# Gelu on four W1 items at once and silu on two W2 items at once, in a fused attention and MLP kernel

## The chip, the core and the metric

The kernel runs on one core of a Trainium2 chip. A core has five engines with their own in-order instruction queues, which meet through semaphores: TensorE (PE, matmuls; PEld are its weight loads), VectorE (DVE), ScalarE (ACT), GpSimd (POOL) and SyncE (SP, which here issues all DMAs). The metric is the device time of one execution in microseconds; lower is better.

## The reference

```python
def _A_ref(x, wqkv, wo):                      # 32 heads of 32, sequence 2048, width 1024
    q, k, v = split(x @ wqkv)
    p = softmax(q @ k.T * 32 ** -0.5)
    return (p @ v) @ wo

def _B_ref(x, w1, b1, w2, b2):                # hidden width 3584
    y = _layernorm(x)
    h = gelu(y @ w1 + b1)                     # tanh form
    return h @ w2 + b2

xn = _layernorm(A_x)
return A_x + _A_ref(xn, ...) * silu(_B_ref(xn, ...))
```

All tensors are bf16, x is 2048 x 1024. Two chains hang on the normalized x: an attention block and an MLP. Their product, added to x, is the output.

## The kernel before

**A planner writes the order.** The kernel does not call the engines directly. Each piece of work is an operation with an engine, a cost, a priority and tokens that it reads and writes (`dve`, `act`, `dma`, `chunk`, lines 580 to 601). `_Plan.run` (line 93) then simulates the engines with these costs and fixes the order of every queue, and `settle` (390) derives the semaphore waits. So a changed cost or dependency can move any instruction behind it. The costs of DVE and ACT are linear in the elements with a fixed part (`c_ps`, `c_f32`, `c_b16`, `c_b4`, `c_act`, `c_acts`, lines 552 to 568).

**Attention** is done for 8 groups of 4 heads (w = 0 to 7), each with 8 blocks of 256 queries and 8 units of 256 keys. A unit is 8 score matmuls on PE (L811, into 6 of the 8 PSUM banks), two exponentials of 128 x 1024 on ACT (L820, tile P), and the matmuls of P with the values (L605). DVE adds up the exponentials for the softmax sums (L837 and L854, tiles PA and PR). Scores have the first claim on PE: other work is placed so that it ends before ACT would run dry, by a guard.

**The MLP** goes through the rows in 8 chunks of 256. Its PE work is cut into items which take one of the other two PSUM banks in turn, together with projections, values and the output projection.

- `make_y` (970) loads x again, normalizes it on DVE and transposes it by DMA into yT.
- A W1 item (`w1_item`, 981; 14 to a chunk) is 16 matmuls for 256 hidden columns. DVE then adds b1 from the PSUM bank into half of a tile xb (L992, 128 x 512), which frees the bank. After every second item the gelu of both is done on 1024 elements per partition: three operations on DVE (L1001 to L1003), a tanh on ACT (L1004), two more on DVE (L1005, L1008). The last writes two of the 20 slots of hT. There are two xb and two ut tiles, so two pairs can be under way.
- A W2 item (`w2_item`, 1014; 4 to a chunk) is 56 matmuls that read the 14 hT slots of its chunk. DVE forms z from the bank (L1029, 128 x 512), ACT takes its tanh (L1033, with an f32 result), DVE forms the product (L1034), and a DMA stores it to a scratch tensor in DRAM (L1036). All three tiles z, zh, g exist twice, in gw.

`seq_mlp` (1043) gives the order: W1 of the first chunk, and then for each chunk its four W2 items with six W1 items of the next chunk between them (2 after each of the first three), and the other eight W1 items of the next chunk. `mlp(10.0, 450.0)` (1113) spreads this over positions among the 512 units of attention. The planner opens a W2 item only when all DVE operations that it depends on have started in the plan, and any item only when its PSUM evacuation waits for nothing but the item itself (lines 295 to 298). Priorities: exponentials go before tanh on ACT (0 and 1) unless a tanh has waited 2500 ns; on DVE bank evacuations have 0, gelu 3, pair sums 3.2.

hT is used for three things: staged x at the start, the hidden values, and at the end staged rows of x and of the stored silu results (lines 1190 to 1203). gw holds normalized x at the start and f32 intermediates in the last rows (1230).

In the last group (w = 7) the output projection items (L1215) run, their results are multiplied with the silu results and added to x on DVE (L1223, L1226), and stored.

Of the kernel before, what the change touches and what calls it, by code (L numbers as in the profile page):

```python
# [6 lines left out]
ACT = mybir.ActivationFunctionType  # L7
ALU = mybir.AluOpType
BF16 = mybir.dt.bfloat16
F32 = mybir.dt.float32  # L10
# [445 lines left out]
def bass_recurrent_scan__mha_block__mixer_channel_mlp__prompt_kernel(  # L456
# [16 lines left out]
    NW1 = FB // 2  # L473
    EPS = 1e-5
    SCALE = 32 ** -0.5
    GC, GA = 0.7978845608028654, 0.044715
# [11 lines left out]
    with ExitStack() as st:  # L488
        def sb(name, shape, dt):
            return st.enter_context(nc.sbuf_tensor(name, list(shape), dt))  # L490

        g_d = nc.dram_tensor("g_scratch", (S, D), BF16).ap()
        o_d = nc.dram_tensor("o_scratch", (HG, 128, S), BF16).ap()

        NP, NPX, NPA, NH, NW1R, NW2R = 10, 16, 3, 20, 3, 4
# [12 lines left out]
        hT = sb("hT", [128, NH, 2, 256], BF16)  # L508
# [3 lines left out]
        w2r = sb("w2r", [128, NW2R, 7, 256], BF16)  # L512
        b2b = sb("b2b", [128, D], BF16)
        b1T = sb("b1T", [128, FB], BF16)
        xb_t = [sb(f"xb{i}", [128, 2, 512], BF16) for i in range(2)]
        ut_t = [sb(f"ut{i}", [128, 2, 512], BF16) for i in range(2)]
        gw = sb("gw", [128, 4096], BF16)
        z_t = [gw[:, i * 2048:i * 2048 + 512] for i in range(2)]
        g_t = [gw[:, i * 2048 + 512:i * 2048 + 1024] for i in range(2)]
        zh_t = [gw[:, i * 2048 + 1024:i * 2048 + 2048].bitcast(F32) for i in range(2)]  # L520
        nt_t = sb("nt", [128, 256], F32)
        nv_t = [sb(f"nv{i}", [128, 256], F32) for i in range(2)]
        nr_t = sb("nr", [128, 8], F32)
# [16 lines left out]
        xnb = [gw[:, i * 1024:(i + 1) * 1024] for i in range(4)]  # L540
        iota_i = ut_t[0][:].rearrange("p a b -> p (a b)")[:, 0:256].bitcast(I32)

        def bank(i, lo=0, hi=512):
            return ps[:, i * 512 + lo:i * 512 + hi]
# [7 lines left out]
        def c_ps(n):  # L552
            return 77 + 1.0417 * n

        def c_f32(n):
            return 67 + 1.0417 * n

        def c_b16(n):
            return 67 + 0.521 * n

        def c_b4(n):
            return 67 + 0.2605 * n
# [4 lines left out]
        def c_acts(n):  # L567
            return 82 + 0.8334 * n
# [11 lines left out]
        def dve(fn, occ, R, W, prio, item=None, extra=()):  # L580
            o = add("DVE", fn, occ, DL, R, W, prio, extra=extra)
            if item is not None:
                linked(o, item)
            return o

        def act(fn, occ, R, W, prio, item=None):
            o = add("ACT", fn, occ, AL, R, W, prio)
            if item is not None:
                linked(o, item)
            return o  # L590
# [4 lines left out]
        def dma(sem, fn, nbytes, R, W, prio=3, extra=(), rate=290.0, occ=430, lat=2500.0):  # L595
            return add("SP", fn, occ, lat, R, W, prio, sem=sem, nbytes=nbytes, extra=extra, rate=rate)
# [148 lines left out]
        def after(tokens, of):  # L745

            got = []
            for x in of:
                w = plan.last_w.get(x)
                got += ([w] if w is not None else []) + plan.readers.get(x, [])  # L750
            for x in tokens:
                plan.readers.setdefault(x, []).extend(got)
# [197 lines left out]
                plan.dense["proj"].append(it)  # L950


        nw2 = {"n": 0}
        ut_n = {"n": 0}
        mq = plan.dense["mlp"]

        def load_w1(p):
# [22 lines left out]

        def w1_item(c, pi):
            p = c * NW1 + pi
            gi, hs, half = p % NW1R, p % NH, pi % 2
            ui = (p // 2) % 2
            it = _Item("mlp")
            for f2 in range(2):
                for dc in range(DC):
                    def fn(e, b, f2=f2, dc=dc):
                        return mm(e, bank(b, f2 * 256, (f2 + 1) * 256), w1r[:, gi, dc, f2 * 128:f2 * 128 + 128], yT[:, dc, :],
                                  dc == 0 and f2 == 0, dc == DC - 1)  # L990
                    chunk(it, fn, Q256, [("w1", gi), ("yT", 0), ("yT", 1)])
            dve(lambda e: e.tensor_tensor(xb_t[ui][:, half].rearrange("p (k t) -> p k t", k=2),  # L992
                                          bank(it.bank).rearrange("p (k t) -> p k t", k=2),
                                          b1T[:, 2 * pi:2 * pi + 2].unsqueeze(2).to_broadcast([128, 2, 256]), op=ALU.add),
                c_ps(512), [("b1",)], [("xb", ui, half)], 0, it)
            if half == 0:
                return it
            xs = [("xb", ui, 0), ("xb", ui, 1)]
            fl = lambda t: t[:].rearrange("p a b -> p (a b)")
            u_ = fl(ut_t[ui])  # L1000
            dve(lambda e: e.tensor_tensor(u_, fl(xb_t[ui]), fl(xb_t[ui]), op=ALU.mult), c_b16(1024), xs, [("ut", ui)], 3)  # L1001
            dve(lambda e: e.tensor_scalar(u_, u_, GA, 1.0, op0=ALU.mult, op1=ALU.add), c_b4(1024), [("ut", ui)], [("ut", ui)], 3)
            dve(lambda e: e.tensor_tensor(u_, u_, fl(xb_t[ui]), op=ALU.mult), c_b16(1024), [("ut", ui)] + xs, [("ut", ui)], 3)  # L1003
            act(lambda e: e.activation(u_, u_, ACT.Tanh, scale=GC), c_acts(1024), [("ut", ui)], [("ut", ui)], 1)  # L1004
            dve(lambda e: e.tensor_scalar_add(u_, u_, 1.0), c_b4(1024), [("ut", ui)], [("ut", ui)], 3)  # L1005
            h0 = (p - 1) % NH
            if h0 + 1 < NH:
                dve(lambda e: e.tensor_tensor(hT[:, h0:h0 + 2].rearrange("p s k t -> p (s k t)"), u_, fl(xb_t[ui]), op=ALU.mult),  # L1008
                    c_b16(1024), [("ut", ui)] + xs, [("h", h0), ("h", h0 + 1)], 3)
            else:  # L1010
                raise AssertionError
            return it

        def w2_item(c, q):
            n = c * 4 + q
            zi = n % 2
            it = _Item("mlp")
            for r in range(4):
                wi = w2slot[(c, q, r)]
                for t2 in range(2):  # L1020
                    for f in range(7):
                        def fn(e, b, r=r, t2=t2, f=f, wi=wi):
                            fb = r * 7 + f
                            hs = (c * NW1 + fb // 2) % NH
                            return mm(e, bank(b, t2 * 256, (t2 + 1) * 256), hT[:, hs, fb % 2, t2 * 128:t2 * 128 + 128],
                                      w2r[:, wi, f, :], r == 0 and f == 0 and t2 == 0, r == 3 and f == 6)
                        chunk(it, fn, Q256, [("w2", wi), ("h", (c * NW1 + (r * 7 + f) // 2) % NH)])
            cs = slice(q * 256, (q + 1) * 256)
            dve(lambda e: e.scalar_tensor_tensor(z_t[zi].rearrange("p (t n) -> p t n", t=2),  # L1029
                                                 bank(it.bank).rearrange("p (t n) -> p t n", t=2), 0.5,  # L1030
                                                 b2b[:, cs].unsqueeze(1).to_broadcast([128, 2, 256]), op0=ALU.mult, op1=ALU.add),
                c_ps(512), [("b2",)], [("z", zi)], 0, it)
            act(lambda e: e.activation(zh_t[zi], z_t[zi], ACT.Tanh, scale=0.5), c_acts(512), [("z", zi)], [("zh", zi)], 1)  # L1033
            dve(lambda e: e.scalar_tensor_tensor(g_t[zi], zh_t[zi], 1.0, z_t[zi], op0=ALU.add, op1=ALU.mult),  # L1034
                c_f32(512), [("zh", zi), ("z", zi)], [("g", zi)], 3)
            dma(f"g{zi}", lambda e: e.dma_start(g_d[c * 256:(c + 1) * 256, cs].rearrange("(t p) n -> p t n", p=128),  # L1036
                                                g_t[zi].rearrange("p (t n) -> p t n", t=2)), 131072,
                [("g", zi)], [("g_d", c, q)])
            return it

        w2slot = {}
# [65 lines left out]
            after([("w2", i)], [("P", 13 + k, h) for k in range(3) for h in range(2) if k * 2048 < (i + 1) * 1792  # L1107
                                and (k + 1) * 2048 > i * 1792])
        after([("h", k) for k in range(NH)], [XS(t) for t in range(NXS)])
        after([(k, i) for i in range(2) for k in ("z", "zh", "g")], [("xnb", t) for t in range(4)])  # L1110

        proj(1, 0)
        mlp(10.0, 450.0)
# [10 lines left out]
        for w in range(HG):  # L1124
# [23 lines left out]
            for qb in range(NQB):  # L1148
                if w == 0 and qb < 2:
                    continue  # L1150
                g = w * NQB + qb
# [35 lines left out]
                for t2 in range(2):  # L1187
                    tb = 2 * qb + t2
                    ri = tb % 3 if tb < 12 else tb - 9
# [9 lines left out]
                    xr, gr = xg[:, 0:1024], xg[:, 1024:2048]  # L1199
# [4 lines left out]
                    for nh in range(2):  # L1204
                        late = qb == NQB - 1
                        it = _Item("wo", 64 * 7 + 8 * qb + 4 * t2 + 2 * nh)
                        i2 = 2 * t2 + nh
                        sl_ = slice(nh * 512, (nh + 1) * 512)
                        if late:
                            most = _Item("wo", it.pos + 64)  # L1210
# [11 lines left out]
                        if not late:  # L1222
# [7 lines left out]
                        xf = gw[:, i2 * 1024:(i2 + 1) * 1024].bitcast(F32)  # L1230
                        dve(lambda e, most=most, gr=gr, sl_=sl_, xf=xf: e.scalar_tensor_tensor(
                            xf, bank(most.bank), 0.5, gr[:, sl_], op0=ALU.mult, op1=ALU.mult),
                            c_ps(512), [("gr", ri, nh)], [("xf", i2)] + [(k, t2) for k in ("z", "zh", "g")], 0, most)
                        dve(lambda e, xr=xr, sl_=sl_, xf=xf: e.tensor_tensor(xf, xf, xr[:, sl_], op=ALU.add),
                            c_f32(512), [("xr", ri, nh)], [("xf", i2)], 2)
                        if i2:
# [84 lines left out]
```

## Time and profile before

| | |
|---|---|
| time, median of 3 runs | 1042.89 us (1042.58 to 1043.29) |
| span of the profiled execution | 1042.1 us, 0.8 us less than that median; its own time with what lies around the span is not given apart |
| ACT busy | 1017.7 us (98%), 1129 instructions |
| PE busy | 1008.8 us (97%) |
| DVE busy | 958.4 us (92%), 1450 instructions |
| mean granted clock of TensorE | 0.998 |
| DMA, mean over the span | 161 GB/s |

The profile is of one execution. Times are microseconds unless marked ns; L820 is line 820 of the kernel. A group of instructions is shown as line, engine, operation, names of the tiles written and read, their shapes, the count, then busy time in us, the mean duration of one in ns, and the idle time of the engine just before them with what ended it. A wait row reads "who waited <- for whom: us in total, times, longest". The chain of work goes back from the last instruction to whatever released each step; its pieces are given by start and length. Matmuls are pipelined, so a busy PE is not PE at its peak.

### The profile page before, as it was taken

The numbers are of one execution on the slowest core, as the hardware profiler recorded it, in microseconds if no ns is written. First come the engines' busy times: TensorE is split into PE (matmuls) and PEld (weight loads), VectorE is DVE, ScalarE is ACT, GpSimd is POOL, SyncE is SP. The second block draws the span as 40 slices with busy tenths as digits, with TensorE's granted clock in tenths as the row PEclk, the third lists the DMA queues.
The fourth block names the chain that finished last, engine by engine and source line by source line (L and its number), as shares of the span: only waits on it lengthen the run. The fifth ranks groups of instructions, "written<-read, shape, count | busy, mean of one in ns | idle before, by whom it ended". The sixth has DMA issues, their size and how long they took to land.

```text
span 1042.1 us, 31753 instructions
## 1 busy us (share of the span) xinstructions
PE 1008.8 (97%) x14179; PEld 640.8 (61%) x14179; DVE 958.4 (92%) x1450; ACT 1017.7 (98%) x1129; POOL 11.0 (1%) x20
## 2 busy tenths in 40 slices
PE   9999899999999999999999999999999999999996
PEld 7555567666665676667665765666657655754442
DVE  8589998999899999998999989999999999878887
ACT  5899999999999999999999999999999999999996
POOL 1200000000000000000000000000000000000000
PEclk9999999999999999999999999999999999999999
DMA  8985558537654577376555674575456753763321
GB/s 198 193 224 145 128 169 226 143 98 204 183 167 127 152 210 217 91 185 181 149 143 157 175 219 128 125 198 169 135 137 195 204 168 121 224 212 111 105 82 52
DMA packets 318200, 168.00 MB, mean 161 GB/s; under 512 B 56688, under 2 KB 306032, under 8 KB 318064
## 3 DMA queue, kind: packets, MB, share of 16 engines
q1 hardware_dynamic: 318064, 165.98, 58.3%
q8 instruction: 111, 1.82, 0.7%
q14 instruction: 25, 0.20, 0.1%
HBM read 146.55 MB, written 12.06 MB: 152 GB/s over the span
## 4 chain that ended last, share of the span: by engine, by line
ACT 89%; PE 4%; DVE 3%; DMA 3%; SPq 0%; issue 0%; POOL 0%
ACT P L820 82%; ACT ut L1004 5%; PE ps L610 3%; ACT gw L1033 2%; DVE stats L761 1%; PE ps L605 1%; PE ps L811 1%; DMA hT<-in_A_x_dram 1%; DMA w2r<-in_B_w_dram 1%; ACT w1r L820 1%; DMA yst<-in_A_x_dram 1%; ACT w2r L820 1%; DMA xnT<-gw 0%; DVE gw L738 0%; DMA yT<-yst 0%
## 5 line engine op out<-in xcount | busy, mean ns | idle before, releaser
L820 ACT ACTIVATE P<-ps 128x1024 bf16<-128x1024 f32 x1012 | 956.6, 1237 | 4.3 <-PE ps L811 4.2
L837 DVE TENSOR_TENSOR PA<-P 128x2048 bf16<-128x2048 bf16 x178 | 216.4, 1219 | 26.3 <-ACT P L820 25.6
L610 PE MATMUL ps<-yT,w1r 128*128 128x256 bf16 x1792 | 227.5, 273 | 1.0 <-DVE xb L992 0.4
L610 PE MATMUL ps<-w2r,hT 128*128 128x256 bf16 x1792 | 222.3, 273 | 0.4 <-DMA w2r<-in_B_w_dram 0.4
L811 PE MATMUL ps<-QKT 32*128 32x256 bf16 x4096 | 203.3, 273 | 18.4 <-ACT P L820 16.7
L854 DVE TENSOR_TENSOR PR<-PR,PA 128x2048 bf16<-128x2048 bf16 x178 | 216.2, 1214 | 1.3
L610 PEld LDWEIGHTS ps<-yT,w1r 128*128 128x128 bf16 x1792 | 163.8, 98 | 51.7 <-issue 27.9
L610 PEld LDWEIGHTS ps<-w2r,hT 128*128 128x128 bf16 x1792 | 163.9, 98 | 48.1 <-issue 29.1
L811 PEld LDWEIGHTS ps<-QKT 32*128 32x128 bf16 x4096 | 60.7, 92 | 152.8 <-ACT P L820 146.6
L605 PE MATMUL ps<-P,V 128*32 128x256 bf16 x4048 | 138.0, 274 | 0.0
L610 PE MATMUL ps<-xnT,wqk 128*128 128x512 bf16 (+1 forms) x552 | 130.4, 365 | 0.2 <-ACT xnT L728 0.2
L605 PEld LDWEIGHTS ps<-P,V 128*32 128x32 bf16 x4048 | 96.1, 96 | 30.6 <-issue 22.8
L610 PE MATMUL ps<-wv,xnT 128*128 128x256 bf16 (+1 forms) x576 | 87.2, 285 | 2.7 <-DVE V L682 1.4
L610 PEld LDWEIGHTS ps<-xnT,wqk 128*128 128x128 bf16 x552 | 48.4, 98 | 51.2 <-issue 13.7
L992 DVE TENSOR_TENSOR xb<-ps,b1T 128x512 bf16<-128x512 f32 x112 | 76.6, 684 | 1.4 <-PE ps L610 1.0
L837 DVE TENSOR_TENSOR PR<-P 128x2048 bf16<-128x2048 bf16 x62 | 75.4, 1215 | 1.4 <-ACT P L820 1.1
L1004 ACT ACTIVATE ut<-ut 128x1024 bf16<-128x1024 bf16 x56 | 70.9, 1266 | 0.0
L610 PEld LDWEIGHTS ps<-wv,xnT 128*128 128x128 bf16 x576 | 52.1, 98 | 27.4 <-issue 11.2
L694 DVE CAST QKT<-ps 128x512 bf16<-128x512 f32 x59 | 40.4, 685 | 2.8 <-PE ps L610 2.4
L1001 DVE TENSOR_TENSOR ut<-xb 128x1024 bf16<-128x1024 bf16 x56 | 38.3, 683 | 0.2
L1003 DVE TENSOR_TENSOR ut<-ut,xb 128x1024 bf16<-128x1024 bf16 x56 | 38.0, 679 | 0.0
L909 DVE STREAM_TRANSPOSE nt<-ps 128x256 f32<-128x256 f32 x64 | 28.4, 443 | 10.3 <-PE ps L605 10.2
(76 smaller groups left out, 564.9 us busy)
## 6 DMA issues: line engine op xcount, KB each, us to landing
w1r<-in_B_w_dram SPq DMA_DIRECT2D x112, 512.0 KB, 4.5
w2r<-in_B_w_dram SPq DMA_DIRECT2D x128, 448.0 KB, 4.4
hT<-in_A_x_dram SPq DMA_DIRECT2D x20, 256.0 KB, 4.0
wqk<-in_A_wqkv_dram SPq DMA_DIRECT2D x16, 256.0 KB, 3.8
yst<-in_A_x_dram SPq DMA_DIRECT2D x16, 256.0 KB, 4.6
g_scratch<-gw SPq DMA_DIRECT2D x32, 128.0 KB, 3.9
o_scratch<-ot SPq DMA_DIRECT2D x56, 64.0 KB, 3.6
xnT<-o_scratch SPq DMA_DIRECT2D x7, 512.0 KB, 5.7
```

Of the source, the lines that this page charges most:

```text
L605: ins = e.matmul(dst(j), lhsT=lhsT(j), rhs=rhs(j), start=start, stop=stop, tile_position=(0, 32 * j), skip_group_check=True)
L610: return e.matmul(dst, lhsT=lhsT, rhs=rhs, start=start, stop=stop, skip_group_check=True)
L694: dve(lambda e: e.tensor_copy(QKT[sl][:, which, tq * 512:(tq + 1) * 512], bank(it.bank)), c_ps(512), [], [(nm, sl, 2 * tq), (nm, sl, 2 * t ...
L811: ins = e.matmul(bank(b0[j], kk * 256, (kk + 1) * 256), lhsT=QKT[sl][32 * j:32 * j + 32, 1, kb * 128:(kb + 1) * 128], rhs=QKT[sl][32 * j:3 ...
L820: x = act(lambda e, h=h: e.activation(Pt[pi][:, 2 * h:2 * h + 2].rearrange("p j k q -> p (j k q)"), ps[:, pr[h] * 1024:(pr[h] + 1) * 1024] ...
L837: return dve(lambda e: e.tensor_tensor(dst[:].rearrange("p u j q -> p (u j) q"), src[:].rearrange("p u j k q -> p (u j) k q")[:, :, 0, :], ...
L854: return dve(lambda e: e.tensor_tensor(fl3(pr), fl3(pr), fl3(PA[i]), op=ALU.add), c_b16(2048), [("PA", i), tok], [tok], 3.2)
L909: dve(lambda e: e.transpose(nt_t[:], bank(pv.bank, 256, 512)), c_ps(256) + 120, [], [("nt",)], prio, pv)
L992: dve(lambda e: e.tensor_tensor(xb_t[ui][:, half].rearrange("p (k t) -> p k t", k=2), bank(it.bank).rearrange("p (k t) -> p k t", k=2), b1 ...
L1001: dve(lambda e: e.tensor_tensor(u_, fl(xb_t[ui]), fl(xb_t[ui]), op=ALU.mult), c_b16(1024), xs, [("ut", ui)], 3)
L1003: dve(lambda e: e.tensor_tensor(u_, u_, fl(xb_t[ui]), op=ALU.mult), c_b16(1024), [("ut", ui)] + xs, [("ut", ui)], 3)
L1004: act(lambda e: e.activation(u_, u_, ACT.Tanh, scale=GC), c_acts(1024), [("ut", ui)], [("ut", ui)], 1)
```

## The change

Gelu now runs on up to four W1 items, and silu on two W2 items.

- The bias add writes x + b1 straight into the item's hT slot; xb is gone. The gelu operations read hT, use a ut tile of twice the size, and the last one writes its result over x in hT.
- Groups are four items (2048 elements per partition), aligned to slots, with a group of two at the end of even chunks and at the start of odd ones. So a chunk has four groups: three of four and one of two.
- z of two W2 items lies side by side. One tanh and one product run on both (1024 elements); the product is written over z, zh exists once, and two DMAs of the old size store the two results.
- Dependencies of the reused space follow the new names.

```diff
-            dve(lambda e: e.tensor_tensor(xb_t[ui][:, half].rearrange("p (k t) -> p k t", k=2),
-                                          bank(it.bank).rearrange("p (k t) -> p k t", k=2),
+            dve(lambda e: e.tensor_tensor(hT[:, hs], bank(it.bank).rearrange("p (k t) -> p k t", k=2),
                                           b1T[:, 2 * pi:2 * pi + 2].unsqueeze(2).to_broadcast([128, 2, 256]), op=ALU.add),
-                c_ps(512), [("b1",)], [("xb", ui, half)], 0, it)
-            if half == 0:
+                c_ps(512), [("b1",)], [("h", hs)], 0, it)
+            if p % 4 != 3 and pi != NW1 - 1 and not (pi == 1 and c % 2):
                 return it
...
+            k = 2 if (pi == NW1 - 1 and p % 4 != 3) or (pi == 1 and c % 2) else 4
+            h0, n = hs - k + 1, k * 512
+            hs_ = [("h", h0 + i) for i in range(k)]
+            ui = geg["n"] % 2
+            geg["n"] += 1
+            x_ = hT[:, h0:h0 + k].rearrange("p s k t -> p (s k t)")
+            u_ = ut_t[ui][:].rearrange("p a b -> p (a b)")[:, 0:n]
+            dve(lambda e: e.tensor_tensor(u_, x_, x_, op=ALU.mult), c_b16(n), hs_, [("ut", ui)], 3)
+            dve(lambda e: e.tensor_scalar(u_, u_, GA, 1.0, op0=ALU.mult, op1=ALU.add), c_b4(n), [("ut", ui)], [("ut", ui)], 3)
+            dve(lambda e: e.tensor_tensor(u_, u_, x_, op=ALU.mult), c_b16(n), [("ut", ui)] + hs_, [("ut", ui)], 3)
+            act(lambda e: e.activation(u_, u_, ACT.Tanh, scale=GC), c_acts(n), [("ut", ui)], [("ut", ui)], 1)
+            dve(lambda e: e.tensor_scalar_add(u_, u_, 1.0), c_b4(n), [("ut", ui)], [("ut", ui)], 3)
+            dve(lambda e: e.tensor_tensor(x_, u_, x_, op=ALU.mult), c_b16(n), [("ut", ui)] + hs_, hs_, 3)
             return it
...
-            act(lambda e: e.activation(zh_t[zi], z_t[zi], ACT.Tanh, scale=0.5), c_acts(512), [("z", zi)], [("zh", zi)], 1)
-            dve(lambda e: e.scalar_tensor_tensor(g_t[zi], zh_t[zi], 1.0, z_t[zi], op0=ALU.add, op1=ALU.mult),
-                c_f32(512), [("zh", zi), ("z", zi)], [("g", zi)], 3)
-            dma(f"g{zi}", lambda e: e.dma_start(g_d[c * 256:(c + 1) * 256, cs].rearrange("(t p) n -> p t n", p=128),
-                                                g_t[zi].rearrange("p (t n) -> p t n", t=2)), 131072,
-                [("g", zi)], [("g_d", c, q)])
+                c_ps(512), [("b2",)], [("z", zi, q % 2)], 0, it)
+            if q % 2 == 0:
+                return it
+            z2 = [("z", zi, 0), ("z", zi, 1)]
+            act(lambda e: e.activation(zh_t, z_t[zi], ACT.Tanh, scale=0.5), c_acts(1024), z2, [("zh",)], 1)
+            dve(lambda e: e.scalar_tensor_tensor(z_t[zi], zh_t, 1.0, z_t[zi], op0=ALU.add, op1=ALU.mult),
+                c_f32(1024), [("zh",)] + z2, z2, 3)
+            for h in range(2):
+                cg = slice((q - 1 + h) * 256, (q + h) * 256)
+                dma(f"g{zi}{h}", lambda e, h=h, cg=cg: e.dma_start(g_d[c * 256:(c + 1) * 256, cg].rearrange("(t p) n -> p t n", p=128),
+                                                       z_t[zi][:, h * 512:(h + 1) * 512].rearrange("p (t n) -> p t n", t=2)), 131072,
+                    [("z", zi, h)], [("g_d", c, q - 1 + h)])
             return it
```

More of the change, by code (lines that the diff above doesn't have):

```diff
@@ L514, in bass_recurrent_scan__mha_block__mixer_channel_mlp__prompt_kernel @@
         b1T = sb("b1T", [128, FB], BF16)
-        xb_t = [sb(f"xb{i}", [128, 2, 512], BF16) for i in range(2)]
-        ut_t = [sb(f"ut{i}", [128, 2, 512], BF16) for i in range(2)]
+        ut_t = [sb(f"ut{i}", [128, 4, 512], BF16) for i in range(2)]
         gw = sb("gw", [128, 4096], BF16)
-        z_t = [gw[:, i * 2048:i * 2048 + 512] for i in range(2)]
-        g_t = [gw[:, i * 2048 + 512:i * 2048 + 1024] for i in range(2)]
-        zh_t = [gw[:, i * 2048 + 1024:i * 2048 + 2048].bitcast(F32) for i in range(2)]
+        z_t = [gw[:, i * 1024:(i + 1) * 1024] for i in range(2)]
+        zh_t = gw[:, 2048:4096].bitcast(F32)
         nt_t = sb("nt", [128, 256], F32)
@@ L950, in proj @@
                 plan.dense["proj"].append(it)
-        nw2 = {"n": 0}
-        ut_n = {"n": 0}
+        nw2, geg = {"n": 0}, {"n": 0}
         mq = plan.dense["mlp"]
@@ L982, in w1_item @@
             p = c * NW1 + pi
-            gi, hs, half = p % NW1R, p % NH, pi % 2
-            ui = (p // 2) % 2
+            gi, hs = p % NW1R, p % NH
             it = _Item("mlp")
@@ L996, in w1_item @@
-            if half == 0:
-                return it
[L998 to L1011, printed above, removed]
+                c_ps(512), [("b1",)], [("h", hs)], 0, it)
@@ L1015, in w2_item @@
             n = c * 4 + q
-            zi = n % 2
+            zi, zo = (n // 2) % 2, (n % 2) * 512
             it = _Item("mlp")
@@ L1028, in w2_item @@
             cs = slice(q * 256, (q + 1) * 256)
-            dve(lambda e: e.scalar_tensor_tensor(z_t[zi].rearrange("p (t n) -> p t n", t=2),
+            dve(lambda e: e.scalar_tensor_tensor(z_t[zi][:, zo:zo + 512].rearrange("p (t n) -> p t n", t=2),
                                                  bank(it.bank).rearrange("p (t n) -> p t n", t=2), 0.5,
                                                  b2b[:, cs].unsqueeze(1).to_broadcast([128, 2, 256]), op0=ALU.mult, op1=ALU.add),
-                c_ps(512), [("b2",)], [("z", zi)], 0, it)
-            act(lambda e: e.activation(zh_t[zi], z_t[zi], ACT.Tanh, scale=0.5), c_acts(512), [("z", zi)], [("zh", zi)], 1)
-            dve(lambda e: e.scalar_tensor_tensor(g_t[zi], zh_t[zi], 1.0, z_t[zi], op0=ALU.add, op1=ALU.mult),
-                c_f32(512), [("zh", zi), ("z", zi)], [("g", zi)], 3)
-            dma(f"g{zi}", lambda e: e.dma_start(g_d[c * 256:(c + 1) * 256, cs].rearrange("(t p) n -> p t n", p=128),
-                                                g_t[zi].rearrange("p (t n) -> p t n", t=2)), 131072,
-                [("g", zi)], [("g_d", c, q)])
+                c_ps(512), [("b2",)], [("z", zi, q % 2)], 0, it)
[10 more added lines that the diff above has]
+                    [("z", zi, h)], [("g_d", c, q - 1 + h)])
             return it
@@ L1109, in bass_recurrent_scan__mha_block__mixer_channel_mlp__prompt_kernel @@
         after([("h", k) for k in range(NH)], [XS(t) for t in range(NXS)])
-        after([(k, i) for i in range(2) for k in ("z", "zh", "g")], [("xnb", t) for t in range(4)])
+        zs = [("z", i, h) for i in range(2) for h in range(2)] + [("zh",)]
+        after(zs, [("xnb", t) for t in range(4)])
         proj(1, 0)
@@ L1232, in bass_recurrent_scan__mha_block__mixer_channel_mlp__prompt_kernel @@
                             xf, bank(most.bank), 0.5, gr[:, sl_], op0=ALU.mult, op1=ALU.mult),
-                            c_ps(512), [("gr", ri, nh)], [("xf", i2)] + [(k, t2) for k in ("z", "zh", "g")], 0, most)
+                            c_ps(512), [("gr", ri, nh)], [("xf", i2)] + zs, 0, most)
                         dve(lambda e, xr=xr, sl_=sl_, xf=xf: e.tensor_tensor(xf, xf, xr[:, sl_], op=ALU.add),
```

## The prediction

> **What bounds the kernel now.** I read the page's busy times first, then the busy time of ScalarE (ACT) inside the long middle stage, then who waits for whom, then the chain of work that ended last.
>
> ```profile
> span 1042.1 us, 31753 instructions
> PE 1008.8 (97%) x14179; PEld 640.8 (61%) x14179; DVE 958.4 (92%) x1450; ACT 1017.7 (98%) x1129; POOL 11.0 (1%) x20
> 53.00:1031.50 978.50, 978.24 (x1081) 1.00 0.58 160
> L820 ACT ACTIVATE P<-ps 128x1024 bf16<-128x1024 f32 x992 | 937.5, 1241 | 0.3 <-PE ps L811 0.2
> L1004 ACT ACTIVATE ut<-ut 128x1024 bf16<-128x1024 bf16 x56 | 70.9, 1266 | 0.0
> L1033 ACT ACTIVATE gw<-gw 128x512 f32<-128x512 bf16 x32 | 26.8, 837 | 0.0
> ```
>
> The third row is a stage table for ACT alone, from 53.0 to 1031.5 us: busy 978.24 of 978.50 us, the granted clock behind it 1.00. The last three rows are ACT's groups in that stretch: the exponentials of attention (L820), the tanh of gelu (L1004) and the tanh of silu (L1033). All idle time before any of them is 0.3 us. PE, DVE and ACT are all above 90% busy, but only ACT has no gaps. So what ACT is spared in this stretch ends the run earlier, as long as the others keep up.
>
> ```profile
> PEld ps L811 <- ACT P L820: 146.6, 485, 1.7
> ACT P L820 <- PE ps L811: 4.2, 6, 1.5
> ```
>
> Columns: total us, times, longest. The score matmuls (L811) wait for ACT 485 times; ACT waits for scores 6 times, nearly all of it in the first 53 us, since only 0.3 us of idle time stands in the stretch above.
>
> What one ACT instruction costs cannot be taken from its duration, because neighbours overlap. The chain of work that ended last gives end to end times:
>
> ```profile
> 53.00 24.75 ACT P L820 x27
> 77.75 0.94 ACT ut L1004
> 78.69 10.08 ACT P L820 x11
> 88.77 0.94 ACT ut L1004
> 89.70 8.25 ACT P L820 x9
> ```
>
> An exponential takes 24.75 / 27 = 0.9167 us. From 53.00 to 89.70 are 36.70 us: 38 exponentials (34.83) and two gelu tanh, so 0.933 us for 1024 elements. Later in the same chain:
>
> ```profile
> 899.84 8.25 ACT P L820 x9
> 908.09 0.51 ACT gw L1033
> 908.60 7.33 ACT P L820 x8
> 915.93 0.51 ACT gw L1033
> ```
>
> From 899.84 to the end of the last row, 915.93 + 0.51 = 916.44, are 16.60 us: 17 exponentials (15.58) and two silu tanh, so 0.508 us for 512 elements. 512 elements more cost 0.425 us, so an instruction without elements costs 0.508 - 0.425 = 0.083 us. That is the price of the change.
>
> **The change part by part.**
>
> *Fewer tanh on ACT.* Before: 8 chunks x 7 pairs = 56 gelu tanh. After: four groups in each chunk, three quads and one pair (in even chunks the pair is last, in odd ones first), so 24 tanh of 2048 and 8 of 1024: 24 instructions fewer for the same elements. Silu: 32 of 512 become 16 of 1024: 16 fewer. Together 40 x 0.083 = 3.3 us. A 2048-wide tanh is not in this trace; by the slope it takes 0.933 + 0.850 = 1.78 us. Each of the end to end means carries a rounding of about 0.005 us, so the fixed part lies between 0.068 and 0.098 and the gain between 2.7 and 3.9 us. I take the middle.
>
> The Trainium skill (ScalarE: Activation LUTs, What ACT_TABLE_LOAD costs) gives an ACTIVATE with immediate scale and bias 186 ns beside its elements and lets back-to-back ones overlap by 93 ns. By it the fixed part is 93 ns and the estimate 40 x 0.093 = 3.7 us, for a time of 1039.2; the chain above measures 83 ns, and the sum goes by that.
>
> *Fewer instructions on DVE.*
>
> ```profile
> L837 DVE TENSOR_TENSOR PA<-P 128x2048 bf16<-128x2048 bf16 x178 | 216.4, 1219 | 26.3 <-ACT P L820 25.6
> L1001 DVE TENSOR_TENSOR ut<-xb 128x1024 bf16<-128x1024 bf16 x56 | 38.3, 683 | 0.2
> L1002 DVE TENSOR_SCALAR ut<-ut 128x1024 bf16<-128x1024 bf16 x56 | 23.4, 419 | 0.1
> L1034 DVE SCALAR_TENSOR_TENSOR gw<-gw 128x512 bf16<-128x512 f32 x32 | 21.8, 682 | 5.0 <-ACT gw L1033 5.0
> ```
>
> A two-input operation goes from 683 ns at 1024 to 1219 at 2048, so its fixed part is 2 x 683 - 1219 = 147 ns. Each quad saves it on three such operations and about the same on two scalar ones: 24 x 5 x 0.147 = 17.6 us, and the 16 merged silu products another 2.4 us. (A 2048-wide scalar operation lies between 419 and 838 ns; with the same fixed part, 691.) About 20 us of DVE goes, but DVE is on no piece of the chain above, so I cost it at nothing. Should DVE be what PE waits for, this is a gain rather than a loss.
>
> *Longer single instructions.* While a 2048-wide gelu operation runs, DVE cannot empty a PSUM bank. It holds 0.536 us longer than now, 72 times for the two-input ones. The pair sums (L837) are already that long and more often. What PE now loses to gelu operations:
>
> ```profile
> PEld ps L605 <- DVE ut L1001: 0.8, 2, 0.4
> PEld ps L610 <- DVE ut L1001: 0.6, 3, 0.2
> PEld ps L610 <- DVE ut L1005: 0.6, 3, 0.2
> ```
>
> 2.0 us on PE's weight loads in 8 waits, next to nothing of it on ACT. I take 0; the upper end is a rival below. Likewise a 1.78 us tanh holds ACT 0.85 us longer at a stretch, in which scores run ahead; the exponentials behind it start no later in sum.
>
> *hT slots taken earlier.* The bias add (L992) now writes its hT slot, so it needs that slot free. Two places. At the start hT stages x:
>
> ```profile
> L738 DVE TENSOR_SCALAR gw<-hT,mv,lnp x16: 526/541/548, 6.9 to 40.6; 128x1024 bf16<-128x1024 bf16 x16
> L992 DVE TENSOR_TENSOR xb<-ps,b1T x112: 674/683/693, 64.8 to 873.9; 128x512 bf16<-128x512 f32 x112
> L610 PE MATMUL ps<-w2r,hT x1792: 272/273/283, 140.6 to 923.2; 128*128 128x256 bf16 x200
> ```
>
> The last read of staged x starts at 40.6 us, the first bias add at 64.8: 24 us of cover, so 0. Later, the ring of 20 slots holds a chunk's 14 and 6 ahead, which is what the item order interleaves; the seventh W1 item of a chunk stands behind the last W2 item of the chunk before anyway. In exchange the limit of two pairs in xb goes. 0, with the boundary below as the doubt.
>
> *Silu and its stores.* The first product of two waits for the second W2 item; its store and the two on SP's queue follow together. Their readers are the loads of w = 7, after the last W2 matmul at 923.2. The last store comes later by 0.43 us of tanh and about 0.54 us of product. What stands behind a store on SP is the next weight loads; PE's whole wait for w2r is
>
> ```profile
> PEld ps L610 <- DMA w2r<-in_B_w_dram: 0.7, 1, 0.7
> ```
>
> so 0, with the same doubt. The number of DMAs is unchanged.
>
> *The order of all queues.* The planner places every instruction anew from its own costs, so all of them move after the first W1 items. I cost this at 0 in the middle: it keeps scores ahead of ACT by a guard, whatever the rest does.
>
> **Sum.** The profiled span of 1042.1 less 3.3 gives 1038.8; the median of the runs lies 0.8 above the span, so 1042.9 - 3.3 = 1039.6.
>
> **The rivals.**
>
> *Scores come late (no difference).* PE's queue is in order. When a bank is not empty or a weight not there, the scores behind wait too, and ACT has little in hand:
>
> ```profile
> 680.02 5.79 DMA w2r<-in_B_w_dram
> 685.85 0.50 PE ps L610 x3
> 650.00:700.00 50.00, 48.83 (x692) 33.14 (x684) 47.33 (x69) 49.74 (x56) 0.00 (x0) 1.00 0.59 152
> ```
>
> The first two rows are of the chain: a w2r block landed at 685.81 and the W2 matmuls resumed. The third is a stage (columns PE, PEld, DVE, ACT busy): ACT lost 0.26 us in it. For: the cover is thin and 72 operations hold DVE 0.54 us longer. Against: only 8 short waits so far. If one long operation in eight cost ACT 0.35 us, 9 x 0.35 = 3.1 us would go, and the time would be 1042.7. It decides from four such events (1.2 us, 1040.8).
>
> *The MLP falls behind and PE sets the end (slower).* W2 of a chunk starts when the last gelu of the chunk is done. At the end of chunk 1:
>
> ```profile
> 233.78 0.68 DVE L992 TENSOR_TENSOR xb<-ps,b1T 128x512 bf16<-128x512 f32 x1
> 246.94 0.65 DVE L1008 TENSOR_TENSOR hT<-ut,xb 128x1024 bf16<-128x1024 bf16 x1
> 247.30 1.59 PE L610 MATMUL ps<-w2r,hT 128*128 128x256 bf16 x13
> ```
>
> 13 us lie between the last bias add and W2; the pair's own operations are 3.8 us of it (three of 0.68, two of 0.42, 0.93 on ACT), the rest is queueing, mostly behind other DVE work. With a quad the own part grows by 3 x 0.54 + 2 x 0.27 + 0.85 = 3.0 us, in the four odd chunks: 12 us if queueing does not stretch it, 36 us if it is stretched threefold, a little less than now (13 / 3.8). PE's cover in the last stage is what its score matmuls wait for ACT there, from 928 us to the end:
>
> ```profile
> PEld ps L811 <- ACT P L820: 24.7, 55, 1.4
> ```
>
> The same row for a stage full of MLP work, 350 to 450 us, and two pieces of the chain at the end:
>
> ```profile
> PEld ps L811 <- ACT P L820: 11.3, 49, 0.4
> 1029.23 1.83 PE ps L610 x8
> 1031.07 1.24 PE ps L605 x40
> ```
>
> The last stage is 1.14 times as long, so at the earlier rate PE would wait 12.9 of its 24.7 us: 11.8 us are to spare. It decides from a delay of 11.8 us that nothing else fills. At 36 us, half filled with projections, it is 18 - 11.8 = 6.2 us: 1045.8. For: in the last two rows PE already does output work back to back when the exponentials end. Against: during the 13 us PE had other work, and less DVE work shortens the queues.
>
> *The merge saves nothing.* If 2048-wide tanh cost twice a 1024-wide one, 1042.9. The two sizes in the trace speak against it.
>
> **How the numbers follow.** Forecast 0.53 (its own range 1038.3 to 1040.8: 3.9 us and 0.6 of luck at the stalls and the end, down to 2.1), late scores 0.26, MLP behind 0.18, nothing saved 0.03. A difference below 0.2%, 2.1 us, is about what a measurement can't tell from none. Faster than 1040.8: 0.54, a little of the late scores being small; within 1040.8 to 1045.0: 0.27; above: 0.19. The range of 8 in 10 runs from 1038.3 to 1045.8, with the end case's middle as its upper end.
>
> **What the profile of the changed kernel would show.** ACT with 40 instructions fewer (1089), 24 gelu tanh at about 1.78 us end to end in the chain, 16 silu tanh at 0.93; ACT busy without a gap from 53 us to about 1028; DVE some 20 us less busy. Late scores would show as idle time before L820, named after PE; a late MLP as a last W2 matmul well after 923 us and PE in the chain long before the last exponential. Idle time before a gelu tanh, named after DVE, would show that a quad's inputs come late on ACT's own queue, which would make the prediction wrong where I saw no risk.

## The result and the profile after

The changed kernel takes 1039.85 us (median of 8 runs, 1039.56 to 1041.55) against 1042.74 us of the kernel before in the same comparison. The ratio is 0.9969 with a 95% interval of 0.996 to 0.9978: 3.2 us less, between 2.3 and 4.2. The profiled executions of `tanh_512` and `after_seed0` further down ran at a lower granted clock (0.849 and 0.947): their profiles are not read, and the first is left out of its comparison, while the second (1049.58 us) is counted in its ratio.

The page's first lines, then ACT alone from the end of the start stage to the last exponential (columns: stage, length, ACT busy), and its groups there:

```profile
span 1037.7 us, 31413 instructions
PE 999.4 (96%) x14064; PEld 637.6 (61%) x14129; DVE 948.0 (91%) x1314; ACT 1014.2 (98%) x1089; POOL 11.0 (1%) x20
52.42:1027.13 974.71, 974.71 (x1040) 1.00 0.58 161
L818 ACT ACTIVATE P<-ps 128x1024 bf16<-128x1024 f32 x992 | 925.3, 1253 | 0.0
L1003 ACT ACTIVATE ut<-ut 128x2048 bf16<-128x2048 bf16 (+1 forms) x32 | 61.2, 1923 | 0.0
L1030 ACT ACTIVATE gw<-gw 128x1024 f32<-128x1024 bf16 x16 | 20.5, 1279 | 0.0
```

ACT has its 40 instructions fewer (1129 to 1089) and still no gap: the same engine sets the time, with less to do. Line numbers have shifted by a few (L818 was L820, L988 was L992). The chain of work shows the new prices:

```profile
52.42 38.50 ACT P L818 x42
90.92 1.79 ACT ut L1003
92.71 12.83 ACT P L818 x14
...
907.01 0.93 ACT gw L1030
907.95 18.33 ACT P L818 x20
```

A 2048-wide tanh costs 1.79 us, a silu tanh of 1024 0.93 us, as forecast (1.78 and 0.933). The exponential stays at 38.50 / 42 = 0.917.

The two profiled spans differ by 4.4 us, more than the medians. The ends of the last exponentials come from these rows of ACT in order of time, before and after:

```profile
999.13 32.40 ACT L820 ACTIVATE P<-ps 128x1024 bf16<-128x1024 f32 x35
```

```profile
993.84 33.29 ACT L818 ACTIVATE P<-ps 128x1024 bf16<-128x1024 f32 x36
```

They are 1031.53 and 1027.13 us. So:

| part of the span | before | after | difference |
|---|---|---|---|
| start, to the exponential at 53.00 or 52.42 | 53.00 | 52.42 | 0.58 |
| from there to the last exponential | 978.53 | 974.71 | 3.82 |
| of it tanh, end to end, summed over the trace | 68.65 | 65.38 | 3.27 |
| of it late exponentials (three of 0.11, 0.17, 0.30; none) | 0.58 | 0 | 0.58 |
| behind the last exponential | 10.5 | 10.6 | 0 |

The 3.27 us are the change. The start holds no instruction that the change touches; its last K copy ends at 48.4 us before and 47.8 after, and anywhere between 46.9 and 49.0 in the other profiles. Late exponentials come and go too (below). What else the rows say, after and then, for the bias add, before:

```profile
ACT P L818 <- PE ps L809: 3.7, 5, 1.1
PEld ps L608 <- DVE gw L1023: 2.9, 4, 1.6
PEld ps L608 <- DVE hT L988: 2.6, 6, 0.6
L608 PE MATMUL ps<-w2r,hT x1792: 272/273/283, 142.5 to 922.4; 128*128 128x256 bf16 x200
```

```profile
PEld ps L610 <- DVE xb L992: 1.2, 2, 0.7
```

PE waits longer for DVE to empty banks: 2.6 us for the bias add (L988) where it was 1.2, and 2.9 us for z (L1023), for which it did not wait before. But ACT does not wait more for scores, 3.7 us against 4.2. The last W2 matmul starts at 922.4 us, 0.8 us earlier than before: the MLP has not fallen behind.

### The profile page after: what moved, and what is told of

It reads as the page before. It is cut to its first block, busy times and chain, and to the rows that moved or that the text cites. A ratio compares the mean times of both kernels' runs of the same rounds, so it can differ in the third digit from the quotient of the medians.

```text
span 1037.7 us, 31413 instructions
## 1 busy us (share of the span) xinstructions
PE 999.4 (96%) x14064; PEld 637.6 (61%) x14129; DVE 948.0 (91%) x1314; ACT 1014.2 (98%) x1089; POOL 11.0 (1%) x20
## 4 chain that ended last, share of the span: by engine, by line
ACT 94%; DVE 3%; PE 2%; DMA 1%; issue 0%; POOL 0%; SPq 0%
ACT P L818 86%; ACT ut L1003 5%; ACT gw L1030 1%; DVE stats L759 1%; PE ps L608 1%; DMA hT<-in_A_x_dram 1%; ACT w1r L818 1%; ACT w2r L818 1%; DMA xnT<-gw 0%; DVE gw L736 0%; PE ps L809 0%; PE ps L603 0%; DVE hT L1247 0%; POOL lnp L767 0%; DVE mv L761 0%
## 5 line engine op out<-in xcount | busy, mean ns | idle before, releaser
L818 ACT ACTIVATE P<-ps 128x1024 bf16<-128x1024 f32 x1012 | 944.4, 1249 | 3.7 <-PE ps L809 3.7
L608 PE MATMUL ps<-xnT,wqk 128*128 128x512 bf16 (+1 forms) x502 | 119.2, 364 | 4.3 <-issue 1.1
L988 DVE TENSOR_TENSOR hT<-ps,b1T 128x512 bf16<-128x512 f32 x112 | 76.6, 684 | 1.5 <-PE ps L608 0.8
L1003 ACT ACTIVATE ut<-ut 128x2048 bf16<-128x2048 bf16 (+1 forms) x32 | 61.2, 1923 | 0.0
L907 DVE STREAM_TRANSPOSE nt<-ps 128x256 f32<-128x256 f32 x64 | 28.3, 443 | 11.8 <-PE ps L603 11.7
L1000 DVE TENSOR_TENSOR ut<-hT 128x2048 bf16<-128x2048 bf16 (+1 forms) x32 | 34.5, 1082 | 0.2
L1005 DVE TENSOR_TENSOR hT<-ut,hT 128x2048 bf16<-128x2048 bf16 (+1 forms) x32 | 34.5, 1079 | 0.1
```

The lines of the kernel that those rows point to most:

```text
L608: return e.matmul(dst, lhsT=lhsT, rhs=rhs, start=start, stop=stop, skip_group_check=True)
L818: x = act(lambda e, h=h: e.activation(Pt[pi][:, 2 * h:2 * h + 2].rearrange("p j k q -> p (j k q)"), ps[:, pr[h] * 1024:(pr[h] + 1) * 1024] ...
L907: dve(lambda e: e.transpose(nt_t[:], bank(pv.bank, 256, 512)), c_ps(256) + 120, [], [("nt",)], prio, pv)
L988: dve(lambda e: e.tensor_tensor(hT[:, hs], bank(it.bank).rearrange("p (k t) -> p k t", k=2), b1T[:, 2 * pi:2 * pi + 2].unsqueeze(2).to_bro ...
L1000: dve(lambda e: e.tensor_tensor(u_, x_, x_, op=ALU.mult), c_b16(n), hs_, [("ut", ui)], 3)
L1005: dve(lambda e: e.tensor_tensor(x_, u_, x_, op=ALU.mult), c_b16(n), [("ut", ui)] + hs_, hs_, 3)
```

## The experiments

The theory: each ACT instruction taken away gives its fixed 0.082 us, and nothing else in the change counts. The rivals: the relief of DVE brings the gain; the new order of the queues brings it by luck; or the MLP's pace matters at the end. Time differences are from the ratio to the kernel before, with its interval.

**One half of the change at a time.**

`gelu_only` is the changed kernel with the silu of before (the main lines; product, store and tiles follow):

```diff
-            if q % 2 == 0:
-                return it
...
-            act(lambda e: e.activation(zh_t, z_t[zi], ACT.Tanh, scale=0.5), c_acts(1024), z2, [("zh",)], 1)
+            act(lambda e: e.activation(zh_t[zi], z_t[zi], ACT.Tanh, scale=0.5), c_acts(512), [("z", zi)], [("zh", zi)], 1)
```

`silu_only` is the kernel before, with xb and gelu on pairs, and the silu of the change (the main lines):

```diff
+            if q % 2 == 0:
+                return it
...
-            act(lambda e: e.activation(zh_t[zi], z_t[zi], ACT.Tanh, scale=0.5), c_acts(512), [("z", zi)], [("zh", zi)], 1)
+            act(lambda e: e.activation(zh_t, z_t[zi], ACT.Tanh, scale=0.5), c_acts(1024), z2, [("zh",)], 1)
```

> Gelu on four items as in the changed kernel, silu on one W2 item as before: 24 tanh fewer on ACT than before, 120 instructions fewer on DVE. If each ACT instruction saved is worth its fixed 0.081 us: 1.9 us less than before, 1040.8. If the gain comes from relief of DVE in proportion to its instructions: 2.9 x 120/136 = 2.6 us, 1040.2. If it is the luck of a new order: anything from 1039 to 1045.

Measured: 0.9983 (0.9974 to 0.9991), 1.8 us less (2.7 to 0.9). ACT's 1.9 us and the 2.6 us of DVE's relief both lie within.

> Gelu on two items as before, silu on two W2 items: 16 tanh fewer on ACT, 16 instructions fewer on DVE. Fixed cost on ACT: 1.3 us less than before, 1041.4. Relief of DVE: 0.3 us, 1042.4. Luck of order: anything.

Measured: 1.0003 (0.9994 to 1.0011): nothing gained, between 0.6 us less and 1.2 us more. ACT's 1.3 us miss; the 0.3 us of DVE's relief would fit, and so would the luck of the order. The trace has the 16 silu tanh at 0.935 us and so the 1.3 us on ACT, but 12.5 us of the run lie behind its last exponential instead of 10.5. Its last W2 matmul, then PE's groups behind the last exponential (from 1030.07 us), and below the same groups of the kernel before (from 1031.53 us):

```profile
L609 PE MATMUL ps<-w2r,hT x1792: 272/273/283, 143.5 to 939.4; 128*128 128x256 bf16 x200
L609 PE MATMUL ps<-wqk,xnT 128*128 128x512 bf16 x9 | 2.4, 379 | 0.2 <-issue 0.2
L609 PE MATMUL ps<-wv,xnT 128*128 128x512 bf16 x6 | 1.8, 379 | 0.0
L609 PE MATMUL ps<-V,xnT 128*128 128x512 bf16 x5 | 1.6, 381 | 0.0
L609 PE MATMUL ps<-yst,xnT 128*128 128x512 bf16 x5 | 1.4, 381 | 0.1
```

```profile
L610 PE MATMUL ps<-yst,xnT 128*128 128x512 bf16 x4 | 1.0, 382 | 1.7 <-DVE xnT L916 1.7
L605 PE MATMUL ps<-P,ones 128*32 128x256 bf16 x16 | 0.8, 273 | 0.0
L605 PE MATMUL ps<-P,V 128*32 128x256 bf16 x12 | 0.7, 273 | 0.0
```

The matmuls of 128x512 with xnT are the output projection (its weights lie in the tiles wqk, wv, V and yst). Before, 4 of them stand behind the last exponential; here 25. The MLP ended 16 us later, and output work that it pushed back was left for the end. This resembles the prediction's slower rival, in a kernel where it was not looked for, with one difference: the rival has PE set the end, and here it is DVE. Two stages from the last exponential on, before and here (columns PE, PEld, DVE, ACT, POOL busy, each with its count, then the granted clock and the DMA), and four pieces of the chain here:

```profile
1031.53:1041.00 9.47, 1.78 (x32) 0.73 (x24) 6.49 (x14) 1.58 (x4) 0.00 (x0) 0.85 0.22 79
1030.07:1041.00 10.93, 6.20 (x41) 2.62 (x41) 9.21 (x18) 1.58 (x4) 0.00 (x0) 0.93 0.17 60
1035.61 0.69 DVE gw L1236
1036.32 0.43 DVE hT L1246
1036.75 0.60 DVE gw L1239
1037.87 0.68 DVE hT L1252
```

PE has 4.4 us more to do there, but from 1030.80 us on the chain is on DVE, short waits aside. DVE has four instructions and 2.7 us more: it empties the late output blocks from PSUM (L1236) and adds x to them (L1239).

**Does the late MLP explain it, and what made it late?** Two runs: the same kernel with the MLP placed earlier, and the changed kernel with gelu on pairs, which differs from `silu_only` only in that x + b1 lies in hT and xb's limit of two pairs is gone. Each has a new order of its queues besides.

`silu_430`, on `silu_only`:

```diff
-        mlp(10.0, 450.0)
+        mlp(10.0, 430.0)
```

`pair_inplace`, on the changed kernel:

```diff
-            if p % 4 != 3 and pi != NW1 - 1 and not (pi == 1 and c % 2):
+            if p % 2 == 0:
...
-            k = 2 if (pi == NW1 - 1 and p % 4 != 3) or (pi == 1 and c % 2) else 4
+            k = 2
```

> Silu on two items, gelu on pairs through xb as before, the MLP spread to position 430 instead of 450. In the run with 450 the last W2 matmul began at 939.4 us against 923.2 before, and 12.5 us instead of 10.5 lay behind the last exponential. If the late MLP ate the 1.3 us saved on ACT: last W2 matmul near 925 us, tail 10.5 us, time 1.3 us less than before, 1041.6. If the silu merge itself costs something: 1043.5 as with 450.

Measured: 0.9986 (0.9978 to 0.9995), 1.5 us less (2.3 to 0.5). Its last W2 matmul:

```profile
L609 PE MATMUL ps<-w2r,hT x1792: 272/273/283, 142.3 to 923.8; 128*128 128x256 bf16 x200
```

The tail behind the last exponential is 10.6 us again, and the gain on ACT appears. So the silu merge costs nothing itself. The 0.3 us of DVE's relief lie outside this interval.

> The changed kernel with gelu on pairs: x in the hT slots, no xb, silu on two items. ACT's instruction count is that of silu on two items alone. If the limit of two pairs in xb held the MLP back there: last W2 matmul near 922 us as in the changed kernel, tail 10.5 us, time 1041.5. If the grouping in fours is what speeds the MLP up: last W2 matmul near 939 us, tail over 12 us, time 1043.5.

Measured: 0.9987 (0.9978 to 0.9996), 1.4 us less (2.3 to 0.4), tail 10.6 us.

```profile
L608 PE MATMUL ps<-w2r,hT x1792: 272/273/283, 153.6 to 922.2; 128*128 128x256 bf16 x200
```

With pairs but without xb the MLP ends at 922.2 us, so the groups of four are not what ends it early. For the freed ring the other traces speak too. The last bias add of the first chunk starts at 113 to 121 us in every kernel without xb and at 125 to 126 us in the four with it. At position 450 the last W2 matmul starts at 919 to 924 us in the six kernels without xb, and at 923.2, 936.5 and 939.4 us in the three with it (before, `before_seed0`, `silu_only`). That xb holds the first W1 items back is shown; since one order with xb ends early as well, how much of the 17 us here is xb's limit and how much the order stays open.

**ACT or DVE?** The changed kernel with the gelu operations of only ACT, or only DVE, put back to 1024 elements.

`tanh_1024`, and `tanh_512` with sz = 512:

```diff
+            sz = 1024
+            us_ = [("ut", ui, i) for i in range(2048 // sz)]
...
-            act(lambda e: e.activation(u_, u_, ACT.Tanh, scale=GC), c_acts(n), [("ut", ui)], [("ut", ui)], 1)
+            for i in range(n // sz):
+                act(lambda e, i=i: e.activation(u_[:, i * sz:(i + 1) * sz], u_[:, i * sz:(i + 1) * sz], ACT.Tanh, scale=GC),
+                    c_acts(sz), [us_[i]], [us_[i]], 1)
```

`dve_1024`, here for the first of the five operations:

```diff
+            hv = [(slice(i * 1024, (i + 1) * 1024), [("ut", ui, i)], hs_[2 * i:2 * i + 2]) for i in range(k // 2)]
...
-            dve(lambda e: e.tensor_tensor(u_, x_, x_, op=ALU.mult), c_b16(n), hs_, [("ut", ui)], 3)
+            for s, w, xs in hv:
+                dve(lambda e, s=s: e.tensor_tensor(u_[:, s], x_[:, s], x_[:, s], op=ALU.mult), c_b16(1024), xs, w, 3)
```

> The changed kernel with each 2048-wide gelu tanh issued as two of 1024: ACT does 24 instructions more than in the changed kernel, DVE the same as there. Fixed cost on ACT: 3.2 - 1.9 = 1.3 us less than before, 1041.4. Relief of DVE: the whole 2.9 us, 1039.8.

Measured: 0.9982 (0.9973 to 0.999), 1.9 us less (2.8 to 1.0). ACT's price says 1.3, DVE's relief 2.9: the interval leaves out the full gain of DVE only by a little.

> The changed kernel with its five DVE gelu operations issued in halves of 1024, 120 more than in the changed kernel, the tanh whole. Fixed cost on ACT: the whole 3.2 us stays, 1039.5, and DVE is busy about 955 us again. Relief of DVE: 0.3 us less than before, 1042.4.

Measured: 0.9969 (0.9957 to 0.9981), the whole 3.2 us. DVE does its old number of gelu instructions:

```profile
PE 999.7 (96%) x14024; PEld 635.5 (61%) x14089; DVE 955.6 (92%) x1434; ACT 1014.5 (98%) x1089; POOL 11.3 (1%) x20
```

DVE is busy 955.6 us, nearly as before, and the gain is all there. The relief of DVE is not its cause.

> The changed kernel with every gelu tanh issued in pieces of 512: 112 instead of 32 gelu tanh, 80 ACT instructions more than in the changed kernel, the same elements and DVE work. Fixed cost of 0.081 us each: 6.5 us above the changed kernel, 1046.3, which is 3.6 us slower than before. If ACT's instruction count is not what moved the time: 1039.8 as the changed kernel.

Measured: 1.0044 (1.003 to 1.0058), 4.6 us slower than before (3.1 to 6.0). The same kernel again:

> The same kernel as with every gelu tanh in pieces of 512, for a clean profile and more times. Fixed cost of 0.081 us: 80 more instructions, 6.5 us above the changed kernel, 3.6 us slower than before, 1046.3, with 0.508 us a piece in the chain and a tail of 10.5 us.

Measured: 1.0029 (1.0017 to 1.004), 3.0 us slower (1.8 to 4.2), with 112 gelu tanh. Its chain:

```profile
88.30 2.03 ACT ut L1006 x4
90.33 12.83 ACT P L818 x14
```

2.03 / 4 = 0.508 us for 512 elements. The three sizes 0.508, 0.935 and 1.789 us (means of end to end times over the traces) lie on one line of 0.081 us and 0.834 ns an element. DVE is relieved here as much as in the changed kernel, and the time is longer than before. By ACT's instruction count against the kernel before: 40 fewer 3.2 us less, 24 fewer 1.8, 16 fewer 1.9, 1.5 and 1.4, 40 more 3.0 and 4.6 us more. Each interval holds the count times 0.082 us; they are too wide to tell 24 from 16. `silu_only`, 16 fewer, stands outside with its later end.

**The luck of the order.**

`before_seed0` and `after_seed0` set the planner's one nonzero seed to zero in the kernel before and in the changed one:

```diff
-        0, 0, 234914347, 0, 0, 0, 0, 0, 0, 0, 0, 0, 0, 0, 0, 0, 0, 0, 0, 0, 0, 0, 0, 0, 0, 0, 0, 0, 0,
+        0, 0, 0, 0, 0, 0, 0, 0, 0, 0, 0, 0, 0, 0, 0, 0, 0, 0, 0, 0, 0, 0, 0, 0, 0, 0, 0, 0, 0,
```

> The kernel before with the planner's one nonzero seed (order noise for 60 to 90 us of its plan) set to zero: another order of all queues after that, the same instructions. If ACT sets the time whatever the order: within 1 us of before, 1042.7. If orders matter by luck: off by 2 us or more.

Measured: 0.9999 (0.999 to 1.0008). Its last W2 matmul starts at 936.5 us, 13 us later than before, and the tail is 10.8 us.

> The changed kernel with the same seed set to zero. If ACT sets the time whatever the order: within 1 us of the changed kernel, 1039.8, and 3.2 us below the kernel before with seed zero. If the gain was the luck of one order: that difference is not near 3.

Measured: 0.9981 (0.9964 to 0.9999), 2.0 us less (3.8 to 0.1), wide for the reason given with the result. Its median of 1040.05 us is 2.7 us below the 1042.75 us of the kernel before with seed zero in the same set. Another order, and the gain is there again.

**How much delay the end can hide.**

`mlp_470`, and `mlp_490` in the same way, on the changed kernel:

```diff
-        mlp(10.0, 450.0)
+        mlp(10.0, 470.0)
```

> The changed kernel with the MLP spread to position 470 instead of 450 of 512, so that its last W2 item ends about 40 us later. By the prediction's cover of 11.8 us on PE in the last stage: slower by up to 28 us, 1068, with PE in the chain long before the last exponential. If PE's spare time is larger than its waits showed, or the positions move the MLP less: 1039.8, no change.

Measured: 0.9974 (0.9965 to 0.9983), 2.7 us less than before; last W2 matmul at 934.2 us (the positions moved it by 12 us, not 40), tail 10.7 us.

> The changed kernel with the MLP spread to position 490. With 470 its last W2 matmul began at 934.2 us (922.4 in the changed kernel) and the time stayed within 0.6 us. If PE's spare time in the last stage is used up at a delay of 12 to 16 us: last W2 matmul near 945 us, tail 13 to 18 us, time 1043 to 1048. If PE has far more to spare: 1040.

Measured: 1.0005 (0.9997 to 1.0014): the whole gain is gone. The last W2 matmul:

```profile
L608 PE MATMUL ps<-w2r,hT x1792: 271/273/284, 142.7 to 934.2; 128*128 128x256 bf16 x200
```

```profile
L608 PE MATMUL ps<-w2r,hT x1792: 272/273/283, 142.8 to 975.3; 128*128 128x256 bf16 x200
```

The first row is of `mlp_470`, the second of `mlp_490`. In the second the tail is 14.5 us, 3.9 more than in the changed kernel. Put together (the tail is the span less the end of the last exponential):

| | last W2 matmul, us | tail, us |
|---|---|---|
| before, changed kernel, `gelu_only`, `tanh_1024`, `dve_1024`, `tanh_512_again`, `pair_inplace`, `silu_430` | 919 to 924 | 10.5 to 10.6 |
| `mlp_470` | 934.2 | 10.7 |
| `before_seed0` | 936.5 | 10.8 |
| `silu_only` | 939.4 | 12.5 |
| `mlp_490` | 975.3 | 14.5 |

**Late scores.** None in the changed kernel, but in `gelu_only`, whose order is another one. Its chain:

```profile
788.31 7.01 DMA w2r<-in_B_w_dram
795.33 0.05 issue
795.37 1.05 PE ps L609 x8
796.42 0.36 PE ps L810 x8
796.78 0.02 issue
796.80 4.71 ACT P L819 x5
```

W2 weights took 7.01 us, PE stood at the head of its queue until 795.33, the scores behind it came late and an exponential lost 1.1 us. With another of 0.86 us at 557, whose cause the chain does not name ("issue"), it is 2.1 us in that profile. `dve_1024` has 1.6 us at 65 to 80 us; there the chain goes over pair sums and a PSUM evacuation on DVE, but in this kernel no gelu operation on DVE is long. With one profile of each kernel it stays open how much of this belongs to the order and how much to the single execution.

## Why the prediction was right

- *The bound.* ACT without a gap sets the time. Right: every comparison with the tail at 10.5 to 10.8 us follows ACT's instruction count within its interval, from 40 fewer to 40 more, and putting DVE back changes nothing that the interval could show.
- *The price, 0.083 us from the chain.* Right: 0.081 to 0.082 with the sizes 512 and 2048 measured, and 3.27 us of tanh less against 3.3. The Trainium skill's 93 ns (ScalarE: Activation LUTs, What ACT_TABLE_LOAD costs) is 11 ns above the measured 82; the times alone would not tell 3.3 from its 3.7 us, the ends of the instructions do.
- *The sum, 1039.6.* The median is 1039.85. So close a hit is partly luck: the difference is known only to lie between 2.3 and 4.2 us, and in the two profiles the start and late exponentials, which the sum put at nothing, differ by 0.58 us each. One step was wrong without harm: that what lies around the span is 0.8 us. Nearly every run's time is 1.7 to 1.9 us above its own span (1039.56 to 1037.7 for the profile after), so the profiled execution of before itself took some 1043.9 us, about 1 us above the median. The sum was formed on the median and did not use it.
- *About 20 us less DVE.* Mis-sized: busy time fell from 958.4 to 948.0, 10.4 us. The 147 ns were taken from durations, but neighbours on DVE overlap. In order of time before:

```profile
174.41 0.68 DVE L992 TENSOR_TENSOR xb<-ps,b1T 128x512 bf16<-128x512 f32 x1
175.01 0.68 DVE L1034 SCALAR_TENSOR_TENSOR gw<-gw 128x512 bf16<-128x512 f32 x1
175.60 0.69 DVE L1001 TENSOR_TENSOR ut<-xb 128x1024 bf16<-128x1024 bf16 x1
```

  Starts are 0.60 us apart for durations of 0.68, so some 0.08 us of each fixed part was never DVE's time: 136 x (0.147 - 0.08) = 9.1 us, near the 10.4. `dve_1024` shows it directly: 120 instructions more cost 955.6 - 948.0 = 7.6 us, 0.063 us each. The same care that was taken with ACT was not taken here. It lay off the path.
- *hT slots and xb at 0.* Right in time here, but freeing xb does more than the prediction saw. Between `silu_only` (939.4) and `pair_inplace` (922.2) the end of the MLP moves by 17 us, by xb's limit and the new order together, and the tail by 1.9 us. Where the MLP ends early enough anyway, as in the kernel before, that is worth 0.
- *The slower rival, MLP behind.* That a late MLP leaves output work for the end is real. A delay of 11.8 us was forecast to be hidden, and the tail grows by 0.2 us at 12 to 13 us of delay, by 1.9 us at 16 and by 3.9 us at 53 (forecast: 6.2 at 36). But the limit was worked out from PE's waits for ACT, and in `silu_only` the chain behind the last exponential is on DVE, which finishes the output blocks. So that the point fits is in part luck, and the price was too high. In the changed kernel the rival did not occur because bias adds came earlier, the last of each chunk by 9 to 15 us. W2 waits longer behind them, 18 to 35 us instead of 12 to 20, a growth well above the 3 us of a quad's own operations. In sum W2 of a chunk starts between 15 us earlier and 5 us later. In chunk 1 the last bias add starts at 225.03 us instead of 233.78, and W2 waits 18.5 us instead of 13.5:

```profile
225.03 0.68 DVE L988 TENSOR_TENSOR hT<-ps,b1T 128x512 bf16<-128x512 f32 x1
243.56 0.28 PE L608 MATMUL ps<-w2r,hT 128*128 128x256 bf16 x1
```

- *The rival of late scores.* It did not occur in the changed kernel's profile. In `gelu_only` it cost 2.1 us, 1.1 of them by weights that landed late; that the longer DVE instructions, which the prediction had in mind, delay scores is shown by no trace here.
- *The merge saves nothing.* Out: 1.79 us is less than 2 x 0.935 = 1.87.

## What to carry to other kernels

Where one engine runs without a gap, price an instruction there from the ends of its neighbours in the chain, not from durations, and multiply: the 3.27 us of tanh that forty instructions fewer saved here were forecast as 3.3. A gain on that engine still has to pass the end of the program; check how much work of the other engines stands behind its last instruction, since a change that delays a side chain by some 15 us can lose there what it saved. A buffer that a change gets rid of may also matter through the limit that it set on the order.

## What the runs showed that was not expected

- ACT's fixed part for this tanh, 81 to 82 ns, is the same at 512, 1024 and 2048 elements and for bf16 and f32 results (0.935 us for both at 1024), while an exponential of 1024 from PSUM takes 0.917 us.
- Merging two silu items, with the same ACT saving as elsewhere, gave nothing until the MLP was moved: 1043.81 us at position 450 (1043.05 for the kernel before in that set), 1041.95 us at 430 (1043.14). At the end of the program DVE, not the saturated ACT, was what the late work had to pass.
